# Four tiles for squares and for gated values, second products two steps later, in a fused convolution and two feed-forward layers

## The chip, the cores and the metric

The kernel runs on one core of a Trainium2 chip. The metric is the device time of one execution in microseconds; the time before is 761.09 us, the median of three runs (760.44 to 761.89). Lower is better.

## The reference

Two sequences of 4160 tokens with 192 channels pass through three layers, all in float32:

```python
# 1: a convolution over the last 7 tokens, with weights per token and head (8 heads)
w = exp(weight_gen - max); w = w / (sum(w) + 1e-9)
x = einsum("bshk,bskhg->bshg", w, last_7_tokens(x))
# 2: feed-forward, 192 -> 1024 -> 192, with the token before mixed in
xk = mu_k * x + (1 - mu_k) * x_prev;  xr = mu_r * x + (1 - mu_r) * x_prev
k = maximum(xk @ w_k, 0)
x = sigmoid(xr @ w_r) * (k * k @ w_v)
# 3: feed-forward, 192 -> 1024 -> 192, with a gate from a convolution over 3 tokens
h = maximum(x @ w_in, 0)
out = (h * sigmoid(conv3(h, conv_w))) @ w_out
```

## The kernel before, in words

**Tiles and steps.** The sequence is cut into ten tiles (256, 220, seven of 476, and 352 tokens), and every tile is worked for both sequences: a tile and a sequence make a unit. In a unit the 1024 hidden channels are done in eight steps of 128, numbered `fi`. A float32 product is made of five matmuls on values split into a high and a low part.

**One step of layer 2** (`moe1`, lines 600 to 636): the first product, five matmuls of `wkA` and `wkB` into a PSUM bank `pa` (two banks); ScalarE takes relu and square in place (`c1`, `c2`) and copies the high part into a tile `s` (`c3`); VectorE subtracts and writes the low part into the same tile (`c4`), which frees the bank; the second product (`go2`, `out_passes`), five matmuls of `wv`, adds the tile `s` into the banks `am` and `ar`. There are two tiles `s`.

**One step of layer 3** (`moe2`, lines 695 to 751): the first product, five matmuls of `wiA` and `wiB` into a bank `pc` (two banks); ScalarE makes `h` (relu) and starts the convolution in the bank (`c1`, `c2`), VectorE adds two taps, ScalarE takes the sigmoid (`c5`), VectorE multiplies by `h` in the bank (`c6`), ScalarE copies the high part into a tile `g` (`c7`) and VectorE writes the low part (`c8`), which frees the bank; the second product, five matmuls of `wo`, adds the tile `g` into the banks `bm` and `br`. There are two tiles `g`.

**Between the layers** `mix_out` multiplies `am` and `ar` by the gate `r` and writes the input `x` of layer 3, and `store` sends the result out. GpSimd does the convolution of layer 1 (`prod`, `tok`) and the low parts of the inputs of layer 2 (`xA`, `mk`). Once for seven of the tiles ScalarE takes an Exp over a 128x2576 block of weights, with a table load before and after.

**What sets the order.** All operations are recorded first, each with a planned time in steps: `at(t, ...)`, where a unit begins at `T + 8 * b` with `T = 16 * i`, step `fi` of layer 2 at `t + fi`, and the same step of layer 3 `LAG` later. Tiles and banks are given out in the order of these planned times (`Ring`, `Shift`). `Program.schedule` then plays the operations through a table of costs: every engine takes, of its operations whose inputs are ready, the one with the lowest planned time. The order that comes of it is fixed in the program; on the chip each engine goes through its list in order and waits where an input is late. `Shift` rings lend tiles after a planned time: for the last steps layer 3 gets the tiles `s` beside `g`, the banks `pa` beside `pc`, and the tiles `mk` beside `h`.

All recorded operations carry line 176 in the profile, so groups are told apart by their tiles.

Of the kernel before, what the change touches and what calls it, by code (L numbers as in the profile page):

```python
# [9 lines left out]
F32R = mybir.dt.float32r  # L10
U32 = mybir.dt.uint32
ACTF = mybir.ActivationFunctionType
ALU = mybir.AluOpType
AX = mybir.AxisListType

NB, SEQ, DM, NH, KS, DFF = 2, 4160, 192, 8, 7, 1024
SIZES = [256, 220] + [476] * 7 + [352]
NTILE = len(SIZES)
STARTS = [sum(SIZES[:i]) for i in range(NTILE)]
NMAX = max(SIZES)  # L20
# [7 lines left out]
PAD = KS - 1  # L28
WIN = KS * DM
NF = DFF // 128  # L30
LAG = 10

DONE = 16 * NTILE + 0.3


def f(ap):
    return ap.bitcast(F32)
# [153 lines left out]
def conv_moe_kernel(ctx: ExitStack, tc: tile.TileContext, xp, wg_first, wg_rest, mus, w_k, w_v, w_r, w_in, conv_w, w_out, out):  # L191
    nc = tc.nc
    prog = Program(nc)
    PE, ACT, DVE, POOL, SP = (prog.engine(e) for e in ("PE", "ACT", "DVE", "POOL", "SP"))
# [8 lines left out]
    def ring(name, n, shape, dtype=F32):  # L203
        return Ring([new(f"{name}{j}", shape, dtype) for j in range(n)])
# [5 lines left out]

    W = NMAX + 4

    class Shift:


        def __init__(self, own, lent, till=None, since=None):
            self.both, self.own, self.tiles, self.till, self.since = Ring(own + lent), Ring(own), own, till, since

        def __call__(self):
            if self.since is None:  # L220
                return self.both() if prog.now < self.till else self.own()
            if prog.now < self.since:
                return self.own()
            if not self.both.n:

                k = self.own.n % len(self.tiles)
                self.both.tiles = self.tiles[k:] + self.tiles[:k] + self.both.tiles[len(self.tiles):]
            return self.both()


    mu = new("mu", [128, 4])
# [15 lines left out]
    stage = new("stage", [128, 4096], U32)  # L247
# [2 lines left out]

    early = x2[1].rearrange("p a b -> p (a b)")
    wb_r = Ring([early[:, :1024].rearrange("p (a b) -> p a b", a=2)])
    g_r = ring("g", 2, [128, 2, W], F32R)
    wz_r = Ring([t.rearrange("p a b -> p (a b)") for t in g_r.tiles])
    rows_r = ring("rows", 2, [128, max(SLOTS) + PAD, DM])
    prod_r = ring("prod", 2, [128, WIN])
    tok_r = ring("tok", 2, [128, max(SLOTS), NB * DM])
# [1 line left out]
    mk_r = ring("mk", 2, [128, NMAX])  # L259
# [1 line left out]
    xA_r = [ring(f"xA{k}", 2, [128, 2, NMAX], F32R) for k in range(2)]  # L261
    xB_r = [ring(f"xB{k}", 3, [128, NMAX], F32R) for k in range(2)]
    r_r = [ring(f"r{k}", 1, [128, NMAX]) for k in range(2)]
    s_r = ring("s", 2, [128, 2, NMAX], F32R)
    h_r = ring("h", 2, [128, W])
    om_r = ring("om", 1, [128, W])

# [2 lines left out]
    soft_at = [sum(slots[:j]) for j in (0, 1, 2, 3, NTILE)]  # L270
# [14 lines left out]
    px_r = Ring([bm_r.tiles[0], br_r.tiles[0]])  # L285
    py_r = Ring(pc_r.tiles)

    pt_r = Shift(pc_r.tiles, pa_r.tiles, since=DONE)
    ht_r = Shift(h_r.tiles, mk_r.tiles, since=DONE)
    gt_r = Shift(g_r.tiles, s_r.tiles, since=DONE)  # L290

    plan = []

    def at(t, fn, hold=0.0):
        plan.append((t, len(plan), fn, hold))
# [304 lines left out]
    def moe1(i, b, fi, t):  # L600
        N = SIZES[i]
        st = {}
        sl = slice(128 * fi, 128 * fi + 128)

        def go():
            p = pa_r()
            st["p"] = p[:, :N]
            mm(st["p"], passes_in(wkA, wkB, xin[i, b, 0, 0], xin[i, b, 0, 1], sl, N))

        def c1():  # L610
            ACT.activation(st["p"], st["p"], ACTF.Relu)

        def c2():
            ACT.activation(st["p"], st["p"], ACTF.Square)

        def c3():
            s = s_r()
            st["s"] = s
            ACT.copy(s[:, 0, :N], st["p"])

        def c4():
            s = st["s"]
            DVE.tensor_tensor(s[:, 1, :N], st["p"], f(s[:, 0, :N]), op=ALU.subtract)

        def go2():
            if fi == 0:
                acc["m"] = am_r.tiles[0]
                acc["r"] = ar_r.tiles[0]
            out_passes(wv, fi, st["s"], N, acc["m"], acc["r"])

        at(t, go)
        at(t + 0.28, c1)
        at(t + 0.45, c2)
        at(t + 0.56, c3)
        at(t + 0.68, c4)
        at(t + 1.25, go2)

    def out_passes(W, fi, s, n, am, ar):
        s0, s1 = s[:, 0, :n], s[:, 1, :n]
# [55 lines left out]
    def moe2(i, b, fi, t):  # L695
        last = i == NTILE - 1
        N = UNIT[i] + (2 if last else 0)
        X = x2[b]
        st = {}
        sl = slice(128 * fi, 128 * fi + 128)  # L700

        def go():
            p = pt_r()
            st["p"] = p
            n = N + 2
            mm(p[:, :n], [(wiA[:, 0, sl], X[:, 0, :n]), (wiA[:, 1, sl], X[:, 0, :n]), (wiA[:, 0, sl], X[:, 1, :n]),
                          (wiB[:, 0, sl], X[:, 2, :n]), (wiB[:, 1, sl], X[:, 3, :n])])

        def c1():
            h = ht_r()  # L710
            st["h"] = h
            ACT.activation(h[:, :N + 2], st["p"][:, :N + 2], ACTF.Relu)

        def c2():
            ACT.activation(st["p"][:, :N], st["h"][:, 1:N + 1], ACTF.Copy, scale=cw[:, 1, fi:fi + 1])

        def tap(k, o):
            DVE.scalar_tensor_tensor(out=st["p"][:, :N], in0=st["h"][:, o:o + N], scalar=cw[:, k, fi:fi + 1],
                                     in1=st["p"][:, :N], op0=ALU.mult, op1=ALU.add)

        def c5():
            ACT.activation(st["p"][:, :N], st["p"][:, :N], ACTF.Sigmoid)

        def c6():
            DVE.tensor_tensor(st["p"][:, :N], st["h"][:, 1:N + 1], st["p"][:, :N], op=ALU.mult)

        def c7():
            g = gt_r()
            st["g"] = g
            ACT.copy(g[:, 0, :N], st["p"][:, :N])  # L730

        def c8():
            g = st["g"]
            DVE.tensor_tensor(g[:, 1, :N], st["p"][:, :N], f(g[:, 0, :N]), op=ALU.subtract)

        def go2():
            if fi == 0:
                acc2["m"] = bm_r()
                acc2["r"] = br_r()
            out_passes(wo, fi, st["g"], N, acc2["m"], acc2["r"])  # L740

        at(t + 0.5, go)
        at(t + 0.78, c1)
        at(t + 0.9, c2)
        at(t + 1.03, lambda: tap(0, 0))
        at(t + 1.17, lambda: tap(2, 2))
        at(t + 1.35, c5)
        at(t + 1.47, c6)
        at(t + 1.66, c7)
        at(t + 1.8, c8)  # L750
        at(t + 2.75, go2)

    def store(i, b, t):
        N = UNIT[i]
# [63 lines left out]
    a = slots[3]  # L818
# [6 lines left out]
    for i in range(NTILE):  # L825
        T = 16 * i
        if i:
            for b in range(NB):
                attention(i, b, T - 22 + 4.5 * b, T - 15 + 4.5 * b + (2 if i == 3 else 0), 1.125, POOL, (25.0 + 8 * b if i == 1 else 0.0, 0.0))
            for u, t in UNITS.get(i, ((0, T - 5), (2, T - 3.7), (1, T + 3))):  # L830
                mixing(i, u, t, 2.5)
        for b in range(NB):
            t = T + 8 * b
            carry(i, b, t + 7)
            for k in range(2):
                gate_r(i, b, k, t + 5.12 + k)
            for fi in range(NF):
                moe1(i, b, fi, t + fi)
                if i:
                    moe2(i, b, fi, t + fi + LAG)  # L840
            mix_out(i, b, t + 8.52)
            if i:
                store(i, b, t + LAG + 10.02)

    heapq.heapify(plan)
    while plan:
# [68 lines left out]
```

## Time and profile before

| | |
|---|---|
| time of three runs | 760.44, 761.09, 761.89 us |
| span of the profiled execution, from its first to its last instruction | 757.9 us |
| median of the runs less this span | 3.2 us |
| TensorE (matmul) busy | 715.6 us, 94% of the span, 3473 matmuls |
| ScalarE busy | 656.6 us, 87% |
| VectorE busy | 606.8 us, 80% |
| GpSimd busy | 492.4 us, 65% |
| granted TensorE clock, mean | 0.992 |

The execution that was profiled has no time of its own beside its span, so the 3.2 us between the span and the median of the runs is taken as what lies around the span. A matmul is pipelined: its record lasts longer than the distance to the next one, so a busy TensorE can still have waited a little. GpSimd is busy nearly without a break until about 510 us, when the convolution of the last tile is done, and rests after that.

### The profile page before, as it was taken

The page shows a single profiled execution, that of the slowest core. Times are in us where ns is not written, and L with a number is a line of the kernel's source. Part 1 is how long each engine was busy: PE and PEld are TensorE (multiplying, and loading weights), DVE is VectorE, ACT ScalarE, POOL GpSimd, SP SyncE. Part 2 cuts the span into 40 slices and gives each one's busy share as a digit, 9 for nine tenths or more (in the row PEclk, how much of TensorE's full clock was granted, in tenths as well). Part 3 has the DMA queues.
Part 4 walks back from the last instruction along what each step waited for, and adds up shares of the span by engine and source line. Part 5 has one row for each costly group of instructions (what it writes and reads, how often), then busy time and mean ns, then how long its engine had stood idle before and what let it go on. Part 6 is the DMA issues. An engine that isn't in the chain of part 4 may idle for free.

```text
span 757.9 us, 10505 instructions
## 1 busy us (share of the span) xinstructions
PE 715.6 (94%) x3473; PEld 607.1 (80%) x3473; DVE 606.8 (80%) x1033; ACT 656.6 (87%) x1388; POOL 492.4 (65%) x350
## 2 busy tenths in 40 slices
PE   4888888997999999999999999999999999999996
PEld 2666777786888888888888788888888888888974
DVE  5756868878997979797979787978797979787887
ACT  2687689989899999899989898999899989898886
POOL 3899999995999999999999999695201000110000
PEclk9899999999999999999999999999999999999999
DMA  7688212101211041013021211020002000200000
GB/s 236 163 262 214 74 53 51 54 20 65 59 53 45 28 124 43 29 53 86 38 72 52 74 48 62 6 72 1 19 2 72 1 20 1 59 3 17 20 1 29
DMA packets 18790, 45.08 MB, mean 59 GB/s; under 512 B 2992, under 2 KB 14256, under 8 KB 18608
## 3 DMA queue, kind: packets, MB, share of 16 engines
q1 hardware_dynamic: 18736, 44.41, 19.8%
q8 instruction: 27, 0.44, 0.2%
q14 instruction: 27, 0.22, 0.1%
HBM read 27.40 MB, written 6.39 MB: 45 GB/s over the span
## 4 chain that ended last, share of the span: by engine, by line
PE 59%; POOL 20%; ACT 11%; DVE 6%; issue 3%; DMA 1%; SPq 0%; ACTq 0%; POOLq 0%; DVEq 0%
PE pa L176 18%; POOL prod L176 16%; PE pc L176 13%; PE bm L176 9%; PE am L176 8%; PE br L176 5%; PE ar L176 5%; ACT pa L176 2%; POOL tok L176 2%; ACT pc L176 2%; DVE pc L176 1%; POOL xA L176 1%; DVE stage L176 1%; ACT h L176 1%; ACT att L176 1%
## 5 line engine op out<-in xcount | busy, mean ns | idle before, releaser
L176 POOL TENSOR_TENSOR prod<-rows,sw 128x1344 f32<-128x1344 f32 x70 | 216.4, 3093 | 12.0 <-DVE sw L176 9.7
L176 DVE SCALAR_TENSOR_TENSOR pc<-h,cw,pc 128x476 f32<-128x476 f32 (+1 forms) x280 | 196.4, 702 | 29.5 <-ACT pc L176 27.0
L176 ACT ACTIVATE pa<-pa 128x476 f32<-128x476 f32 (+3 forms) x324 | 162.6, 504 | 38.2 <-PE pa L176 34.4
L176 POOL TENSOR_TENSOR prod<-prod 128x576 f32<-128x576 f32 (+1 forms) x132 | 161.6, 1224 | 8.8
L176 PE MATMUL am<-s,wv 128*128 128x476 f32 (+3 forms) x480 | 145.4, 362 | 8.3 <-ACT s L176 8.2
L176 PE MATMUL bm<-g,wo 128*128 128x476 f32 (+1 forms) x417 | 138.2, 378 | 4.1 <-ACT g L176 3.6
L176 PE MATMUL pa<-xA,wkA 128*128 128x476 f32 (+3 forms) x480 | 122.8, 360 | 3.6 <-DVE s L176 1.8
L176 DVE TENSOR_TENSOR pc<-h,pc 128x476 f32<-128x476 f32 (+1 forms) x140 | 90.0, 643 | 42.5 <-ACT pc L176 42.1
L176 POOL TENSOR_TENSOR xA<-mk,xA 128x476 fp32r<-128x476 f32 (+2 forms) x36 | 40.2, 1124 | 119.6 <-ACT xA L176 119.6
L176 PE MATMUL pc<-x,wiA 128*128 128x478 f32 (+1 forms) x420 | 115.4, 376 | 0.6 <-DVE g L176 0.5
L176 DVE TENSOR_TENSOR s<-pa,s 128x476 fp32r<-128x476 f32 (+3 forms) x162 | 94.9, 586 | 25.2 <-ACT s L176 23.0
L176 PE MATMUL ar<-s,wv 128*128 128x476 f32 (+3 forms) x320 | 109.4, 353 | 0.0
L176 PEld LDWEIGHTS am<-s,wv 128*128 128x128 f32 x480 | 86.3, 188 | 24.8 <-ACT s L176 14.1
L176 PE MATMUL br<-g,wo 128*128 128x476 f32 (+1 forms) x278 | 104.1, 375 | 0.0
L176 DVE TENSOR_TENSOR g<-pc,g 128x476 fp32r<-128x476 f32 (+1 forms) x137 | 87.6, 640 | 17.1 <-ACT g L176 16.6
L176 PEld LDWEIGHTS pa<-xA,wkA 128*128 128x128 f32 x480 | 84.8, 190 | 18.5 <-DVE s L176 3.9
L176 ACT ACTIVATE pc<-h,cw 128x476 f32<-128x476 f32 (+1 forms) x140 | 92.4, 660 | 1.6
L176 PEld LDWEIGHTS bm<-g,wo 128*128 128x128 f32 x417 | 76.9, 188 | 18.5 <-ACT g L176 6.4
L176 ACT ACTIVATE h<-pc 128x478 f32<-128x478 f32 (+1 forms) x140 | 79.8, 570 | 12.0 <-PE pc L176 9.1
L176 PE MATMUL pa<-xB,wkB 128*128 128x476 f32 (+3 forms) x320 | 88.8, 356 | 0.0
L176 PEld LDWEIGHTS pc<-x,wiA 128*128 128x128 f32 x420 | 76.2, 188 | 13.5 <-DVE g L176 2.5
L176 ACT CAST s<-pa 128x476 fp32r<-128x476 f32 (+3 forms) x162 | 83.5, 517 | 2.7 <-PE ar L176 0.8
(134 smaller groups left out, 1110.7 us busy)
## 6 DMA issues: line engine op xcount, KB each, us to landing
rows<-in_x_dram SPq DMA_DIRECT2D x14, 960.0 KB, 4.6
xB<-rm SPq DMA_DIRECT2D x28, 119.0 KB, 2.3
xB<-mk SPq DMA_DIRECT2D x28, 119.0 KB, 2.3
out_dram<-om SPq DMA_DIRECT2D x14, 238.0 KB, 2.0
rows<-in_x_dram SPq DMA_DIRECT2D x4, 768.0 KB, 6.0
rows<-in_x_dram SPq DMA_DIRECT2D x2, 864.0 KB, 4.4
out_dram<-att SPq DMA_DIRECT2D x14, 119.0 KB, 2.2
stage<-in_moe_w_v_dram SPq DMA_DIRECT2D x4, 384.0 KB, 4.6
```

Of the source, the lines that this page charges most:

```text
L176: getattr(self.real[eng], method)(*a, **k)
```

## The change

Layer 2 and layer 3 get four tiles `s` and four tiles `g`. Second products are planned two steps later in both layers (`S_LAG` 1.25 to 3.25, `G_LAG` 2.75 to 4.75), with `mix_out` and `store` moved by the same, and layer 3 starts one step later behind layer 2 (`LAG` 10 to 11). From tile 7 on, the gated value is written to a tile in SBUF (`q_r`, two tiles in the unused part of `stage`) and not back to its bank, and GpSimd makes the low part of it in place of VectorE. `Grow` replaces `Shift` for lending tiles, and lends the banks `pa` and the tiles `mk` 0.3 steps earlier. The scratch for DMAs is set to 1024 bytes.

```diff
-LAG = 10
-
-DONE = 16 * NTILE + 0.3
+LAG = 11
+
+S_LAG, G_LAG = 3.25, 4.75
+DONE = 16 * NTILE + S_LAG - 0.95
+ALONE = 7
...
+    class Grow:
+
+        def __init__(self, tiles, *more):
+            self.tiles, self.n, self.more = list(tiles), 0, list(more)
 
         def __call__(self):
...
+            while self.more and prog.now >= self.more[0][0]:
+                k = self.n % len(self.tiles)
+                self.tiles = self.more.pop(0)[1] + self.tiles[k:] + self.tiles[:k]
+                self.n = 0
+            self.n += 1
+            return self.tiles[(self.n - 1) % len(self.tiles)]
...
-    g_r = ring("g", 2, [128, 2, W], F32R)
-    wz_r = Ring([t.rearrange("p a b -> p (a b)") for t in g_r.tiles])
+    g_r = ring("g", 4, [128, 2, W], F32R)
+    wz_r = Ring([t.rearrange("p a b -> p (a b)") for t in g_r.tiles[:2]])
...
-    s_r = ring("s", 2, [128, 2, NMAX], F32R)
+    s_r = ring("s", 4, [128, 2, NMAX], F32R)
...
-    pt_r = Shift(pc_r.tiles, pa_r.tiles, since=DONE)
-    ht_r = Shift(h_r.tiles, mk_r.tiles, since=DONE)
-    gt_r = Shift(g_r.tiles, s_r.tiles, since=DONE)
+    spare = f(stage)[:, 2 * (soft_at[4] - soft_at[3]) * NH:]
+    q_r = Ring([spare[:, j * W:(1 + j) * W] for j in (0, 1)])
+    pt_r = Grow(pc_r.tiles, (16 * NTILE, pa_r.tiles))
+    ht_r = Grow(h_r.tiles, (16 * NTILE, mk_r.tiles))
+    gt_r = Grow(g_r.tiles, (DONE, s_r.tiles))
...
-        at(t + 1.25, go2)
+        at(t + S_LAG, go2)
...
         def c6():
-            DVE.tensor_tensor(st["p"][:, :N], st["h"][:, 1:N + 1], st["p"][:, :N], op=ALU.mult)
+            st["q"] = q_r() if i >= ALONE else st["p"]
+            DVE.tensor_tensor(st["q"][:, :N], st["h"][:, 1:N + 1], st["p"][:, :N], op=ALU.mult)
...
-            ACT.copy(g[:, 0, :N], st["p"][:, :N])
+            ACT.copy(g[:, 0, :N], st["q"][:, :N])
...
-            DVE.tensor_tensor(g[:, 1, :N], st["p"][:, :N], f(g[:, 0, :N]), op=ALU.subtract)
+            (POOL if i >= ALONE else DVE).tensor_tensor(g[:, 1, :N], st["q"][:, :N], f(g[:, 0, :N]), op=ALU.subtract)
...
-        at(t + 2.75, go2)
+        at(t + G_LAG, go2)
...
-            mix_out(i, b, t + 8.52)
+            mix_out(i, b, t + S_LAG + 7.27)
             if i:
-                store(i, b, t + LAG + 10.02)
+                store(i, b, t + LAG + G_LAG + 7.27)
...
-    nc = _bacc.Bacc("TRN2", target_bir_lowering=False, num_devices=1)
+    nc = _bacc.Bacc("TRN2", target_bir_lowering=False, num_devices=1, dynamic_dma_scratch_size=1024)
```

TensorE's list has the same matmuls in both kernels, in another order. In the middle of the program (tile 4; the number after a tile's name tells the buffer, `s_103` and `s_104` are the two tiles `s`) it reads before:

```order
L176 MATMUL pa_110<-xA_91,wkA 128x476 x3
L176 MATMUL pa_110<-xB_96,wkB 128x476 x2
L176 MATMUL am<-s_103,wv 128x476 x2
L176 MATMUL ar<-s_103,wv 128x476
L176 MATMUL am<-s_103,wv 128x476
L176 MATMUL ar<-s_103,wv 128x476
L176 MATMUL pc_112<-x_1_75,wiA 128x478 x3
L176 MATMUL pc_112<-x_1_75,wiB 128x478 x2
L176 MATMUL bm<-g_78,wo 128x476 x2
L176 MATMUL br<-g_78,wo 128x476
L176 MATMUL bm<-g_78,wo 128x476
L176 MATMUL br<-g_78,wo 128x476
```

Here a second product reads the square of the step just before. Behind the change the same place (`s_105` to `s_108` are the four tiles `s`) reads:

```order
L178 MATMUL pa_114<-xA_93,wkA 128x476 x3
L178 MATMUL pa_114<-xB_98,wkB 128x476 x2
L178 MATMUL am<-s_105,wv 128x476 x3
L178 MATMUL ar<-s_105,wv 128x476 x2
L178 MATMUL pc_115<-x_1_75,wiA 128x478 x3
L178 MATMUL pc_115<-x_1_75,wiB 128x478 x2
L178 MATMUL bm<-g_77,wo 128x476 x2
L178 MATMUL br<-g_77,wo 128x476
L178 MATMUL bm<-g_77,wo 128x476
L178 MATMUL br<-g_77,wo 128x476
L178 MATMUL am<-s_106,wv 128x476 x2
L178 MATMUL ar<-s_106,wv 128x476
```

The second products now read squares that are three steps old. Counted through the list, from the last matmul of a step's first product to its second product there were about 24 matmuls in layer 2 and 42 in layer 3 in the middle of the program, and there are now about 65 and 85. From the last `wv` matmul of a unit to the first `wiA` matmul of the same unit there were 42, and there are now 25.

ScalarE's list around the large Exp (`sw` 128x2576, in tile 3) reads before:

```order
L176 CAST s_103<-pa_110 128x476
L176 ACTIVATE pc_112<-pc_112 128x476
L176 ACTIVATE h_105<-pc_111 128x478
L176 ACTIVATE pc_111<-h_105,cw 128x476
L176 CAST g_78<-pc_112 128x476
L176 ACT_TABLE_LOAD
L176 ACTIVATE sw<-sw 128x2576
L176 COPY att_85<-pa_110 128x476
L176 ACTIVATE pa_109<-pa_109 128x476
L176 ACT_TABLE_LOAD
L176 ACTIVATE pc_111<-pc_111 128x476
```

And behind the change:

```order
L178 CAST s_105<-pa_113 128x476
L178 ACTIVATE h_110<-pc_116 128x478
L178 CAST g_77<-pc_115 128x476
L178 ACTIVATE pc_116<-h_110,cw 128x476
L178 ACT_TABLE_LOAD
L178 ACTIVATE sw<-sw 128x2576
L178 ACTIVATE pa_113<-pa_113 128x476
L178 CAST rm_91<-mk_89 128x476
L178 ACT_TABLE_LOAD
L178 ACTIVATE pc_116<-pc_116 128x476
L178 ACTIVATE r_103<-pa_114 128x476
```

The copies of the inputs of tile 3 (`att`, `xA`) now stand ahead of the Exp, and at the Exp two more tiles `s` and two more tiles `g` hold values whose second products are still to come.

VectorE's list at the end of the program reads before:

```order
L176 TENSOR_TENSOR g_78<-pa_110,g_78 128x354
L176 TENSOR_TENSOR pc_111<-h_105,pc_111 128x354
L176 SCALAR_TENSOR_TENSOR pc_112<-h_106,cw,pc_112 128x354
L176 TENSOR_TENSOR g_77<-pc_111,g_77 128x354
L176 TENSOR_TENSOR pc_112<-h_106,pc_112 128x354
L176 TENSOR_TENSOR s_103<-pc_112,s_103 128x354
L176 TENSOR_TENSOR att_86<-br,att_86 64x353
```

And behind the change:

```order
L178 TENSOR_TENSOR stage<-mk_89,pa_113 128x354
L178 SCALAR_TENSOR_TENSOR pa_114<-mk_90,cw,pa_114 128x354
L178 SCALAR_TENSOR_TENSOR pc_116<-h_110,cw,pc_116 128x354 x2
L178 TENSOR_TENSOR stage<-mk_90,pa_114 128x354
L178 TENSOR_TENSOR stage<-h_110,pc_116 128x354
L178 TENSOR_TENSOR att_88<-br,att_88 64x353
```

The low parts (`g<-pc,g`, `s<-pc,s`) are gone from VectorE's list: in tiles 7 to 9 there are 48 of them on GpSimd's, each reading `stage`, the tile of the gated value. Behind the last first product of layer 2 (`wkB`) TensorE's list had 130 matmuls, 33 of them ahead of the first matmul of the last unit's layer 3; it now has 160, with 69 ahead.

## Rows read from the trace of the kernel before

**Rows 1.** The page: span.
```profile
span 757.9 us, 10505 instructions
```

**Rows 2.** Windows: length, busy us of PE, PEld, DVE, ACT, POOL (instructions); PEclk, DMA, GB/s.
```profile
0.00:80.00 80.00, 60.97 (x309) 46.86 (x309) 50.98 (x110) 50.72 (x142) 62.45 (x49) 0.96 0.74 212
80.00:176.00 96.00, 88.32 (x477) 75.01 (x478) 77.53 (x135) 83.09 (x196) 92.47 (x66) 1.00 0.15 49
200.00:720.00 520.00, 516.85 (x2450) 444.76 (x2449) 428.60 (x696) 473.78 (x952) 323.49 (x226) 1.00 0.14 41
511.68:587.18 75.50, 75.22 (x354) 64.57 (x354) 61.84 (x99) 69.19 (x138) 19.06 (x15) 1.00 0.09 23
```

**Rows 3.** Chain that ended last, at 250 us: start, us, what.
```profile
250.13 1.08 PE pa L176 x5
```

**Rows 4.** Waits of weight loads (PEld), 200 to 720 us: us, times, longest.
```profile
PEld am L176 <- ACT s L176: 5.0, 8, 0.8
PEld pa L176 <- DVE s L176: 2.1, 8, 0.3
PEld pa L176 <- DVE mk L176: 1.4, 1, 1.4
PEld br L176 <- ACT g L176: 0.7, 2, 0.4
```

**Rows 5.** The same, 80 to 176 us.
```profile
PEld am L176 <- ACT s L176: 2.1, 3, 0.9
PEld bm L176 <- ACT g L176: 1.9, 3, 0.8
PEld bm L176 <- DVE g L176: 1.3, 1, 1.3
```

**Rows 6.** Timeline around the Exp: start, us, engine, instruction.
```profile
177.46 1.28 ACT L176 ACT_TABLE_LOAD   x1
178.75 2.36 ACT L176 ACTIVATE sw<-sw 128x2576 f32<-128x2576 f32 x1
182.02 1.28 ACT L176 ACT_TABLE_LOAD   x1
185.31 1.01 PE L176 MATMUL am<-s,wv 128*128 128x476 f32 x2 [4.03 <-ACT s L176]
```

**Rows 7.** Windows around the Exp and of the last unit, columns as in group 2.
```profile
177.40:181.10 3.70, 3.70 (x20) 3.06 (x18) 1.48 (x3) 3.67 (x4) 0.91 (x2) 1.00 0.08 29
185.30:190.00 4.70, 4.70 (x16) 4.01 (x17) 4.22 (x8) 3.72 (x8) 2.69 (x3) 0.64 0.22 71
...
731.30:753.40 22.10, 19.61 (x98) 14.93 (x96) 20.13 (x42) 17.05 (x42) 0.00 (x0) 1.00 0.04 13
```

**Rows 8.** Groups on DVE, 731.3 to 753.4 us: xcount, busy us, mean ns, idle before.
```profile
L176 DVE TENSOR_TENSOR s<-pc,s 128x354 fp32r<-128x354 f32 x3 | 1.6, 523 | 0.7 <-ACT s L176 0.5
...
L176 DVE TENSOR_TENSOR s<-pa,s 128x354 fp32r<-128x354 f32 x2 | 1.0, 520 | 0.0
```

**Rows 9.** Groups by shape, 560 to 757 us.
```profile
L176 POOL TENSOR_TENSOR xA<-mk,xA 128x352 fp32r<-128x352 f32 x4 | 3.8, 951 | 42.1 <-ACT xA L176 42.1
L176 ACT CAST g<-pc 128x354 fp32r<-128x354 f32 x9 | 4.1, 458 | 1.6 <-DVE pc L176 1.6
L176 ACT CAST xA<-mk 128x352 fp32r<-128x352 f32 x4 | 1.9, 474 | 0.1
```

**Rows 10.** Timeline from the last wv matmul of a unit to its layer 3.
```profile
398.66 0.38 PE L176 MATMUL ar<-s,wv 128*128 128x476 f32 x1
...
402.35 0.65 DVE L176 TENSOR_TENSOR x<-ar,x 64x476 fp32r<-64x476 f32 x1
...
407.75 0.80 PE L176 MATMUL pc<-x,wiA 128*128 128x478 f32 x3
```

**Rows 11.** Timeline: low parts on GpSimd for tile 6, and their reader.
```profile
428.24 2.41 POOL L176 TENSOR_TENSOR mk<-mk,rm 128x476 fp32r<-128x476 f32 x2
...
436.83 0.59 PE L176 MATMUL pa<-xB,wkB 128*128 128x476 f32 x2
```

More of the change, by code (lines that the diff above doesn't have):

```diff
@@ L211, in conv_moe_kernel @@
     W = NMAX + 4
-    class Shift:
-        def __init__(self, own, lent, till=None, since=None):
-            self.both, self.own, self.tiles, self.till, self.since = Ring(own + lent), Ring(own), own, till, since
+    class Grow:
+        def __init__(self, tiles, *more):
+            self.tiles, self.n, self.more = list(tiles), 0, list(more)
         def __call__(self):
[L220 to L228, printed above, removed]
+            while self.more and prog.now >= self.more[0][0]:
[4 more added lines that the diff above has]
+            return self.tiles[(self.n - 1) % len(self.tiles)]
     mu = new("mu", [128, 4])
```

## The prediction

> **What bounds the kernel now.** I read the page first, then windows by stage, the waits of TensorE's weight loads, the timeline at the one long wait, and the last unit by itself.
>
> The span is 757.9 us [rows 1]; the median of the runs is 3.2 us longer, and I add that at the end. From 200 to 720 us TensorE is busy for 516.85 of 520 us at the full clock (1.00, the 2.4 GHz level), ScalarE for 473.78 [rows 2]. One product of five matmuls takes 1.08 us there [rows 3], 0.216 us a matmul. So in two thirds of the span the bound is TensorE's own rate, and the change, which leaves the number of matmuls as it is, can win only what TensorE waits for. There are four such places.
>
> First, small waits in this stretch: weight loads of second products waited 5.0 us for a square (`am <- ACT s`) and 0.7 us for a gated value, and those of first products 2.1 us for a bank that VectorE had to free and 1.4 us for an input [rows 4]. Second, 80 to 176 us, with the same kinds of wait: 2.1, 1.9 and 1.3 us on squares and gated values [rows 5], while TensorE is busy for 88.32 of 96 us [rows 2]. Third, one long stall: at 177.46 us ScalarE loads a table, takes the Exp, and loads the first table again until 183.3 us. TensorE had 20 matmuls in hand, then waited 4.03 us for a square [rows 6, 7]. After the wait its granted clock is 0.64 on the mean of 185.3 to 190 us, part of it at the 1.2 GHz level, and 16 matmuls take 4.70 us [rows 7]; at 0.216 us [rows 3] they would take 3.46. The stall costs 4.03 + 1.24 = 5.3 us. Fourth, the last unit: from 731.3 to 753.4 us VectorE is busy for 20.13 of 22.1 us, ScalarE for 17.05, and TensorE's 98 matmuls [rows 7] at 0.216 x 356/476 = 0.16 us need only 16. There VectorE is the bound.
>
> The first 80 us (TensorE 60.97 of 80, DMA share 0.74 [rows 2]) are loads and the conversion of weights.
>
> **Second products two steps later, four tiles.** By the two lists, about 65 matmuls lie between a first product and its second product in layer 2 (24 before), 85 in layer 3 (42 before). At 0.216 us that is 14 us in place of 5.2, and 18 in place of 9. ScalarE is busy for 69.19 us of a tile's 75.5 [rows 2], so a chain of three or four of its instructions is late by fractions of a microsecond, never by 9.
>
> From 200 to 720 us the 5.7 us of waits on second products should go. What is late next is the bank: `pa` and `pc` still have two banks each, the chain that frees them is untouched, and a wait on a square now hides part of the wait on the bank that follows it. I give 1.2 us back to the banks: 4.5 us won. Bounds: all 5.7 won; nothing won, if every wait moves to a bank.
>
> From 80 to 176 us the rows on second products add up to 5.3 us. The steps are shorter there, and the banks turn over faster against the same chain, so I take 2 us, with bounds of 0 and 5.3.
>
> At the Exp the new list of ScalarE has the inputs of tile 3 done before, and three squares and three gated values are waiting for their second products. Counted from the first product that ScalarE reads last before its table load, 36 matmuls stand in TensorE's list up to the first that needs a result from behind the Exp (the bank of the gate `r`). ScalarE has three instructions between that product and the table load; at 0.6 us each, an estimate from the copies' 458 ns on 354 columns [rows 9], that is 1.8 us or 8 matmuls. 28 are left, 6.0 us. From the table load to the second table's end took 5.84 us [rows 6], and a sigmoid and `r` follow, 1.2 us by the same estimate: a wait of some 1 us, and about 1 us more on the squares right behind. So 3.3 of 5.3 us go; with a shorter wait the clock should not fall as far. I take 3.5 us, with bounds of 0 (ScalarE reaches the Exp late, with its tiles drained) and 5.3.
>
> **`LAG`, `mix_out`, and the end.** Between a unit's last `wv` matmul and its first `wiA` matmul lie 25 matmuls, 5.4 us, in place of 42. The chain in between (VectorE, ScalarE, VectorE) took from 399.04 to 403.00 us, 4.0 us, and TensorE came to its reader only at 407.75 [rows 10]. The last part of `x` is read by the fifth matmul, 0.9 us later: 2.3 us are left. I price it at nothing; the 25 matmuls hide it. If they don't, it is the rival on the other side.
>
> After the last first product of layer 2 there are 160 matmuls, not 130, so it comes 30 x 0.16 = 4.8 us earlier, with 69 matmuls and not 33 until the last unit's layer 3. That is a shift of the same work, at nothing. In the last unit ten low parts leave VectorE, at 0.52 us (two of four rows stand here) 5.2 of 20.13 us [rows 7, 8]; 14.9 are left. ScalarE's 17.05 us are the bound then. With the same ratio of window to busiest engine (22.1 / 20.13) the window is 18.9 us: 3.2 less. The chain at the very end gets longer: a low part takes about 0.95 us on GpSimd [rows 9], not 0.52, and the last two come one behind the other: 0.4 + 0.5 us. The end wins 2.3 us; I take 2. Bounds: 4 us (VectorE's idle goes with its work), and a loss of 1, when each part is late by its longer time.
>
> [...]
>
> The copy of the high part now reads SBUF: 474 ns against 458 [rows 9], 10 x 0.016 = 0.2 us in the last unit, and hidden in TensorE's work in tiles 7 to 9 before. [...]
>
> **GpSimd's list, queues, scratch.** GpSimd's low parts for tiles 4 to 6 stand one convolution product earlier in its list than before, so they keep up with a TensorE that is a few us earlier: for tile 6 they ended at 430.65 us and were read, after a DMA, at 436.83 [rows 11]. Low parts for tile 2 stand behind two more weight products (2.3 us), and GpSimd's list ahead of them is the same. `store` moves with its product, and SP only issues DMAs. [...] I price these at nothing, with 2 us either way for the order of the first 80 us.
>
> **Sum.** 4.5 + 2 + 3.5 + 2 = 12 us. 757.9 - 12 = 745.9 us of span, and with 3.2 around it 749.1 us: I say 749.
>
> **Rivals.**
> Banks take the waits over: nothing is won from 80 to 176 and from 200 to 720 us, only at the Exp and the end: 761.1 - 5.5 = 755.6, 756 us. For it speak the 2.1 us on banks, against it that these are under half of the waits on squares [rows 4]. 0.16.
> More goes than I count: all of the 5.7, 5.3 and 5.3 us, 4 at the end, 2 in the first 80 us, 22 us: 739. 0.09.
> GpSimd's parts stand on the path of the end: each of the last ten is 0.43 us longer than on VectorE [rows 8, 9], 4.3 us lost in place of 2 won: 755. Against it: four tiles let the parts of neighbouring steps overlap, and GpSimd has nothing else to do there. 0.05.
> No change: the Exp still drains TensorE, banks take the small waits, and the longer parts eat the end's gain: 760 to 762. 0.07.
> Slower, by one mechanism: `mix_out` no longer fits under 25 matmuls. It costs nothing up to 2.3 us of delay, then 1 us a unit for each further us, in 17 units; at 3.5 us of delay 17 x 1.2 = 20 us, 761.1 - 12 + 20 = 769. It decides the sign from 3.0 us of delay on. For it speaks that VectorE and ScalarE have longer chains of other steps in their lists by then, against it that VectorE is idle for 13.7 of 75.5 us [rows 2]. 0.06.
>
> **Chances.** The forecast has 0.57. A measurement of this kernel tells about 0.2%, 1.5 us, from no change. Faster by more: 0.57 + 0.16 + 0.09 + 0.05 less a little for the weak end of the first rival, 0.86. Within: 0.08. Slower: 0.06. The forecast's own range is 744 to 754; the range reaches from the second rival to past the first and the third, with the 2 us on the first 80 us: 739 to 758.
>
> **What would show it.** Right: `am <- ACT s` on TensorE's weight loads from 200 to 720 us falls from 5.0 us to under 1; no wait of over 2 us and a clock of 0.9 or more in the windows at the Exp; a tile takes under 75.2 us; in the last unit ScalarE, not VectorE, is the busiest, and the window from its first `wiA` matmul to its last `wo` matmul is near 20 us. Wrong: `pa <- DVE s` or `pc <- DVE` waits grow by what `am` loses; waits of TensorE on `x` in every unit; low parts of `g` on GpSimd that TensorE waits for.

## The result, and the profile after

The changed kernel takes 749.06 us, the median of 4 runs (747.3 to 749.3); the kernel before took 761.24. The ratio is 0.984, with a 95% interval of 0.982 to 0.985. The profiled execution has a span of 747.5 us against 757.9, which is 10.4 less; its own time, 749.3 us, is 1.8 us longer than its span. In all runs of the two kernels and their variants below this difference is 1.7 to 2.2 us. So the execution that was profiled before took some 759.7 us, faster than the median, and of the 12.2 us between the two medians the two traces hold 10.4.

The windows of the changed kernel answer to [rows 2], the last of them to the third of [rows 7]; the columns are those of [rows 2]:

```profile
0.00:80.00 80.00, 60.52 (x315) 46.87 (x316) 50.95 (x111) 51.48 (x145) 62.40 (x50) 0.98 0.74 212
80.00:176.00 96.00, 89.46 (x480) 76.09 (x480) 78.55 (x138) 84.26 (x200) 91.91 (x64) 0.98 0.16 50
176.00:200.00 24.00, 22.89 (x104) 18.41 (x103) 21.92 (x35) 23.14 (x42) 16.74 (x14) 1.00 0.29 81
200.00:720.00 520.00, 517.32 (x2463) 446.94 (x2462) 411.21 (x666) 471.07 (x960) 365.12 (x262) 1.00 0.14 40
724.10:743.05 18.95, 16.85 (x93) 14.44 (x91) 14.50 (x29) 15.76 (x39) 9.40 (x10) 1.00 0.05 15
```

From 200 to 720 us TensorE is hardly busier than before (517.32 against 516.85). The last unit, from its first `wiA` matmul to its last `wo` matmul, is 3 us shorter, with 93 matmuls in its window in place of 98, and VectorE in it went from 20.13 to 14.50 us.

Fixed windows hide a shift, so I also set the two traces beside each other at equal work: each matmul counts with its columns, and the table gives the time at which the same share of all products has been started.

| stretch (time in before, us) | ahead at its end, us | won in it, us |
|---|---|---|
| start to 173 | 1.1 | 1.1 |
| 173 to 220, with the Exp | 6.0 | 4.9 |
| 220 to 301 | 5.8 | -0.2 |
| 301 to 341 | 1.9 | -3.9 |
| 341 to 665 | 4.4 | 2.5 |
| 665 to 707 | 5.4 | 1.0 |
| 707 to the end | 10.4 | 5.0 |

Where the order of the two lists differs, neighbouring points of this measure scatter, by a microsecond or two in the first 130 us. One loss of 3.9 us stands among the gains. The waits of weight loads from 200 to 720 us, as in [rows 4], show what ended them:

```profile
PEld pa L178 <- DVE s L178: 4.5, 9, 2.5
PEld pc L178 <- DVE g L178: 3.0, 12, 0.6
...
PEld pc L178 <- DVE stage L178: 0.7, 2, 0.5
```

`am <- ACT s`, 5.0 us before, is gone from the list. Waits on banks that VectorE frees are now the largest, and 2.5 us of them are one single wait. Before, the waits of `pc` on VectorE were these:

```profile
PEld pc L176 <- DVE g L176: 0.8, 3, 0.3
```

So `pa <- DVE s` grew by 2.4 us and `pc <- DVE` by 2.9, together 5.3 us, as much as `am` lost. The prediction had named this as a sign of being wrong. Around the single wait of 2.5 us, GpSimd, VectorE and TensorE stand like this (three timelines of the changed kernel: start, duration, instruction, and in brackets how long its engine had been idle and who ended that):

```profile
330.07 3.09 POOL L178 TENSOR_TENSOR prod<-rows,sw 128x1344 f32<-128x1344 f32 x1
333.12 2.34 POOL L178 TENSOR_TENSOR xA<-mk,xA 128x476 fp32r<-128x476 f32 x2
```

```profile
331.38 0.65 DVE L178 TENSOR_TENSOR pc<-h,pc 128x476 f32<-128x476 f32 x1
334.35 0.71 DVE L178 SCALAR_TENSOR_TENSOR mk<-att,onemu,pa 128x476 f32<-128x476 f32 x1 [2.33 <-POOL xA L178]
334.98 0.65 DVE L178 TENSOR_TENSOR s<-pa,s 128x476 fp32r<-128x476 f32 x1
```

```profile
335.68 1.27 PE L178 MATMUL pa<-xA,wkA 128*128 128x476 f32 x3 [2.09 <-DVE s L178]
```

Read from the top: GpSimd takes a weight product of 3.09 us before the low parts of `xA`. VectorE wants to write `mk`, of which there are two tiles, and GpSimd has yet to read the one whose turn it is. Behind that write, in VectorE's list, stands the low part of a square, and the bank that it frees is the one TensorE needs. When the wait ends, at 335.7 us, the granted clock falls: it is 0.50 from 336.05 to 339.46 us, and five matmuls over 476 columns, from 336.75 to 338.73 us, take 1.98 us there, where one such product took 1.08 before [rows 3]. These are 1.2 columns a ns, the prediction's 1.2 GHz level; its 2.4 is twice that, an estimate by the shares of 0.50 and 1.00. Two windows have the clock at 0.76 and 0.82 on the mean:

```profile
334.00:338.00 4.00, 2.32 (x7) 1.97 (x8) 3.62 (x6) 1.97 (x4) 4.00 (x5) 0.76 0.26 60
338.00:342.00 4.00, 4.00 (x17) 3.44 (x16) 2.06 (x4) 3.29 (x7) 3.92 (x5) 0.82 0.75 169
```

At the Exp two waits of TensorE's weight loads are left, 1.7 us together, and the clock stays at 1.00 (the window from 176 to 200 us above; 0.64 behind the stall before [rows 7]):

```profile
188.33 0.51 PEld L178 LDWEIGHTS pa<-xA,wrA 128*128 128x128 f32 x3 [1.27 <-ACT r L178]
189.71 0.30 PEld L178 LDWEIGHTS am<-s,wv 128*128 128x128 f32 x2 [0.44 <-ACT s L178]
```

### The profile page after: what moved, and what is told of

Same layout as the page of the kernel before. It is cut to its first block, busy times and chain, and to the rows that moved or that the text cites. A ratio compares the mean times of both kernels' runs of the same rounds, so it can differ in the third digit from the quotient of the medians.

```text
span 747.5 us, 10554 instructions
## 1 busy us (share of the span) xinstructions
PE 711.2 (95%) x3473; PEld 606.9 (81%) x3473; DVE 581.2 (78%) x985; ACT 650.0 (87%) x1388; POOL 546.7 (73%) x398
## 4 chain that ended last, share of the span: by engine, by line
PE 48%; POOL 35%; ACT 6%; DVE 4%; issue 4%; DMA 2%; SPq 0%; ACTq 0%; POOLq 0%; DVEq 0%
POOL prod L178 28%; PE pa L178 15%; PE pc L178 10%; PE bm L178 7%; PE am L178 6%; PE br L178 5%; PE ar L178 4%; POOL tok L178 3%; POOL xA L178 2%; DVE pc L178 1%; ACT pa L178 1%; POOL mk L178 1%; DMA stage<-in_moe_w_in_dram 1%; DMA stage<-in_moe_w_k_dram 1%; DVE mk L178 1%
## 5 line engine op out<-in xcount | busy, mean ns | idle before, releaser
L178 ACT ACTIVATE pa<-pa 128x476 f32<-128x476 f32 (+4 forms) x326 | 163.3, 504 | 29.6 <-PE pa L178 26.0
L178 PE MATMUL am<-s,wv 128*128 128x476 f32 (+3 forms) x480 | 142.0, 356 | 2.9 <-ACT s L178 2.8
L178 PE MATMUL bm<-g,wo 128*128 128x476 f32 (+1 forms) x414 | 135.2, 379 | 2.1 <-ACT g L178 1.8
L178 POOL TENSOR_TENSOR g<-stage,g 128x476 fp32r<-128x476 f32 (+1 forms) x42 | 48.5, 1156 | 96.3 <-ACT g L178 76.0
L178 PE MATMUL pc<-x,wiA 128*128 128x478 f32 (+1 forms) x414 | 113.4, 379 | 0.9 <-ACT x L178 0.4
L178 DVE TENSOR_TENSOR s<-pa,s 128x476 fp32r<-128x476 f32 (+3 forms) x160 | 93.8, 586 | 21.6 <-ACT s L178 20.2
L178 DVE TENSOR_TENSOR pc<-h,pc 128x476 f32<-128x476 f32 x96 | 62.8, 654 | 26.9 <-ACT pc L178 26.0
L178 PE MATMUL pc<-x,wiB 128*128 128x478 f32 (+1 forms) x276 | 81.7, 377 | 0.0
```

The costliest lines, as they stand in the source:

```text
L178: getattr(self.real[eng], method)(*a, **k)
```

## The experiments

Each ratio is to runs of the kernel before that were taken together with this one, with its 95% interval; the changed kernel's is 0.9836 (0.9822 to 0.9850). The medians of the kernel before in these groups lie between 760.65 and 761.24 us, so a difference of two medians from two groups can be off by some 0.6 us, and the ratios are the better comparison.

| kernel | median, us | ratio |
|---|---|---|
| tiles_alone | 762.68 | 1.0018 (1.0006 to 1.0031) |
| lags_alone | 766.22 | 1.0076 (1.0060 to 1.0092) |
| low_parts_alone | 755.69 | 0.9925 (0.9906 to 0.9944) |
| no_low_parts | 754.76 | 0.9902 (0.9881 to 0.9924) |
| own_tile_alone | 753.80 | 0.9903 (0.9885 to 0.9921) |
| third_mk | 749.46 | 0.9841 (0.9816 to 0.9867) |
| four_mk | 744.47 | 0.9788 (0.9771 to 0.9804) |
| four_mk_before | 758.87 | 0.9977 (0.9968 to 0.9987) |
| no_exp_before | 757.85 | 0.9961 (0.9945 to 0.9976) |
| no_exp_after | 747.16 | 0.9824 (0.9809 to 0.9839) |
| four_mk_from_6 | 747.04 | 0.9823 (0.9808 to 0.9839) |
| four_mk_four_q_from_6 | 744.17 | 0.9783 (0.9759 to 0.9807) |

### Which part carries how much

**tiles_alone**, against the changed kernel (the smaller scratch stays):

```diff
-LAG = 11
+LAG = 10
-S_LAG, G_LAG = 3.25, 4.75
+S_LAG, G_LAG = 1.25, 2.75
-ALONE = 7
+ALONE = 99
```

> Four tiles for squares and for gated values with the lags of before and no low parts on GpSimd; the lists of the engines are nearly those of before (75 rows of TensorE's 2038 differ). Theory (the lag carries the gain, the tiles only make room for it): am still follows its square by 1.25 steps, so TensorE's waits for the cast of the square, 5.0 us in 200 to 720, and the stall at the Exp stay. Time 759 to 761. Rival (the tiles carry it): casts run ahead by themselves, those waits fall by half or more, and the time is 753 to 756.

Measured: 762.68 us. The waits on squares from 200 to 720 us stand as they did in [rows 4]:

```profile
PEld am L178 <- ACT s L178: 5.0, 8, 0.8
```

Four tiles, together with `Grow` and the smaller scratch, win nothing: 0.2% is lost. What each of the three does alone is not shown.

**lags_alone**, against the changed kernel:

```diff
-ALONE = 7
+ALONE = 99
-g_r = ring("g", 4, [128, 2, W], F32R)
+g_r = ring("g", 2, [128, 2, W], F32R)
-s_r = ring("s", 4, [128, 2, NMAX], F32R)
+s_r = ring("s", 2, [128, 2, NMAX], F32R)
```

> The changed lags with two tiles for squares and two for gated values, and no low parts on GpSimd. Theory (lag needs the tiles): with two tiles a cast waits until the second product of two steps before has read its tile, and that product now stands two steps later; TensorE waits for squares and gated values all through, and the time is 765 to 800. Rival (the lag alone does it, since the order of TensorE's list is what counts): 753 to 756, as no_low_parts with 754.9.

Measured: 766.22 us, within what was expected, but not by the mechanism that I gave. With two tiles step f + 2 writes its square, in the recorded order, ahead of the second product of step f, which then reads the later step's square: this part of the computation is changed. TensorE does not wait for squares all through (2.1 us from 200 to 720) but for banks:

```profile
PEld pa L178 <- DVE s L178: 10.2, 16, 2.8
```

With another flow of data its time says nothing on lag by itself; it shows only that this lag needs more than two tiles.

**low_parts_alone**, against the changed kernel:

```diff
-LAG = 11
+LAG = 10
-S_LAG, G_LAG = 3.25, 4.75
+S_LAG, G_LAG = 1.25, 2.75
-    g_r = ring("g", 4, [128, 2, W], F32R)
+    g_r = ring("g", 2, [128, 2, W], F32R)
-    s_r = ring("s", 4, [128, 2, NMAX], F32R)
+    s_r = ring("s", 2, [128, 2, NMAX], F32R)
```

> The kernel before with one part of the change: from tile 7 on GpSimd makes the low parts of the gated values, out of a tile of their own; two tiles and the lags of before. Theory (the parts act on different places): the last unit shortens by 2 to 4 us, the Exp stall and the waits for the square before tile 7 stay; time 757 to 759. Rival (GpSimd's low part of 0.95 us is too late for second products that follow by 2.75 steps): TensorE waits for g in tiles 7 to 9, and the time is 761 or more.

Measured: 755.69 us, a gain of 5.4, more than the 2 to 4 expected. At equal work nothing is won before 665 us (0.5 behind), and 5.3 us are won from there on. In its last unit VectorE has 16.36 us of work in place of 20.13 [rows 7], and the window is 20.25 us:

```profile
728.40:748.65 20.25, 18.57 (x95) 14.98 (x95) 16.36 (x33) 17.55 (x43) 10.36 (x11) 1.00 0.05 15
```

**no_low_parts**, against the changed kernel:

```diff
-ALONE = 7
+ALONE = 99
```

> The changed kernel with the low parts of the gated values on VectorE in all tiles; tiles and lags as changed. Theory (GpSimd's low parts give the end): 18 to 20 low parts of 0.52 us return to VectorE in the last unit, where it is the busiest, and the last unit goes from 19.0 us back towards the 21.9 us of before; in tiles 7 and 8 TensorE's wait for the square returns to 0.7 us per tile. Time 752 to 753. Rival (the two steps of lag give the end): the last unit stays under 20 us and the time at 749 to 750.

Measured: 754.76 us, the median of five runs (a sixth, of 1166.74 us, is left out), 5.7 slower than the changed kernel and beyond the expectation. Its last unit takes 22.9 us, and the clock in it is not full:

```profile
726.40:749.30 22.90, 18.62 (x89) 16.31 (x87) 18.42 (x38) 15.64 (x37) 0.00 (x0) 0.85 0.04 13
```

One single wait is 3.5 us of this window, and it is on ScalarE: TensorE needs the bank `bm`, out of which ScalarE has still to copy the result of the unit before (`om`).

```profile
PEld bm L178 <- ACT om L178: 3.5, 1, 3.5
```

At equal work this trace keeps its distance to the changed kernel's from 640 to 724 us, and its whole loss comes behind that, where this wait and the slow clock stand. So the theory has the place right, but this run does not separate VectorE's load from that wait.

Tiles with lag are thus worth 6.4 us (761.12 - 754.76) and low parts on GpSimd 5.4 to 5.7; the sum, 12, is what both bring together. They act in different places.

**own_tile_alone**, against the changed kernel:

```diff
-            (POOL if i >= ALONE else DVE).tensor_tensor(g[:, 1, :N], st["q"][:, :N], f(g[:, 0, :N]), op=ALU.subtract)
+            DVE.tensor_tensor(g[:, 1, :N], st["q"][:, :N], f(g[:, 0, :N]), op=ALU.subtract)
```

> The changed kernel with VectorE making the low parts in all tiles, but from tile 7 on still out of a tile of its own in SBUF, so that the bank of PSUM is free before the low part. Theory (VectorE's work is what counts at the end): like no_low_parts, 754 to 755.5, last unit near 22.9 us. Rival (the bank that comes free earlier is what counts): the last unit stays under 20.5 us and the time is 749 to 751.

Measured: 753.80 us, just under the theory's range, and a ratio of 0.9903 against 0.9902 for no_low_parts. The bank that comes free earlier is worth nothing that can be measured. The profiled run, 750.4 us, is its fastest and looks like the rival: its last unit took 20.2 us, not 22.9, at a clock of 1.00, and against the changed kernel it loses 2.4 us in the last unit. Its clock over the whole span is 0.992, that of the five other runs 0.983 to 0.987, so a good part of what they take longer goes with the clock. Where they lost it is not shown.

### The loss at 330 us

**third_mk**, against the changed kernel; `spare` is the part of `stage` that lies idle from tile 4 on:

```diff
+    mk_own = mk_r.tiles
+    mk_r = Grow(mk_own, (16 * 4, [spare[:, 2 * W:2 * W + NMAX]]))
-    ht_r = Grow(h_r.tiles, (16 * NTILE, mk_r.tiles))
+    ht_r = Grow(h_r.tiles, (16 * NTILE, mk_own))
```

> The changed kernel, and from tile 4 on a third mk tile, laid in the part of stage that lies idle then; GpSimd's list keeps its prod instructions where they are. Theory (the two mk tiles): the 4 us that the changed kernel loses at 330 to 340 us come from VectorE's write of mk waiting 2.33 us for GpSimd's xA, which stands behind a prod of 3.09 us, with the square that frees a bank queued behind that write. With a third tile that wait goes, the granted clock there stays at 0.98 to 1.00, and the time falls by 3 to 4 us, to 745 to 746. Rival (GpSimd itself is late): the low part of xA is needed by TensorE soon after, so the wait moves to TensorE for xA and the time stays at 748 to 749.

Measured: 749.46 us, so the theory's time failed. The trace says why: at equal work the kernel is 2.4 us ahead of the changed one from 359 to 399 us, and level again at 420. A unit writes two `mk`, and two units follow each other closely, so four writes stand together; in the next tile the fourth of them met the same thing:

```profile
412.83 0.71 DVE L178 SCALAR_TENSOR_TENSOR mk<-att,onemu,pa 128x476 f32<-128x476 f32 x1 [3.09 <-POOL xA L178]
```

**four_mk**, against third_mk:

```diff
-    mk_r = Grow(mk_own, (16 * 4, [spare[:, 2 * W:2 * W + NMAX]]))
+    mk_r = Grow(mk_own, (16 * 4, [spare[:, 2 * W + j * NMAX:2 * W + (j + 1) * NMAX] for j in (0, 1)]))
```

> As third_mk, with a fourth mk tile beside the third. In third_mk the wait of VectorE at 330 us shrank from 2.33 to 0.6 us and TensorE was 2.4 us ahead from there to 399 us; at 412 us, in the next tile, the fourth write of mk met the same thing (3.09 us for xA behind a prod), and all was lost again. Theory (each write of mk that reuses a tile too soon can lose 2 to 4 us): with four tiles, as many as the two units next to each other write, both losses go, the clock stays at 1.00 through 326:346 and 400:420, and the time is 745 to 746. Rival (GpSimd's list is simply late, and any slack is used up by the next reader, rm or xA or TensorE itself): TensorE waits for xA or xB there instead, and the time stays at 748.5 to 749.5.

Measured: 744.47 us, a little beyond the theory's range, and 4.6 under the changed kernel (3.7 by the two ratios). No write of `mk` waits any more, and from 200 to 720 us TensorE is never idle:

```profile
200.00:720.00 520.00, 520.00 (x2496) 451.47 (x2495) 415.71 (x676) 474.35 (x969) 366.45 (x264) 1.00 0.14 40
```

**four_mk_before**, against the kernel before:

```diff
+    spare = f(stage)[:, 2 * (soft_at[4] - soft_at[3]) * NH + 2 * W:]
+    mk_own = mk_r.tiles
+    mk_r = Shift(mk_own, [spare[:, j * NMAX:(j + 1) * NMAX] for j in (0, 1)], since=16 * 4)
-    ht_r = Shift(h_r.tiles, mk_r.tiles, since=DONE)
+    ht_r = Shift(h_r.tiles, mk_own, since=DONE)
```

> The kernel before with four mk tiles from tile 4 on, and nothing else; TensorE's list is the same row for row. VectorE's writes of mk waited once for xA there, 1.2 us (3.5 us in three waits in the changed kernel). Theory (the loss on mk was brought by the change, whose list puts xA behind a prod): four tiles win 1 to 2 us here, 759 to 760, against 4.6 in the changed kernel. Rival (two mk tiles cost the same in both, and the change only showed it): 756 to 757.

Measured: 758.87 us, 2.1 less, against 4.6 in the changed kernel; by the ratios it is 0.23% against 0.48%. Before, one write of `mk` waited, at 400 to 425 us:

```profile
DVE mk L176 <- POOL xA L176: 1.2, 1, 1.2
```

With four tiles the trace wins 1.3 us between 422 and 463 us. So, as far as these intervals tell, close to half of what four tiles win was lost before the change already, and the change brought the other half.

### The price of the Exp

**no_exp_before** and **no_exp_after** are the kernel before and the changed one without one line:

```diff
-    at(45.3, lambda: ACT.activation(sm[3][0][:, a:], sm[3][0][:, a:], ACTF.Exp))
```

> The kernel before without the Exp over 128x2576 and the two table loads around it; the later tiles then use weights that are not normalised. In the changed kernel leaving it out gave 1.9 us. Theory (the stall costs its wait and the slow clock behind it, 4.03 + 1.24 us): 5 to 6 us less, 755 to 756. Rival (part of the stall comes back as later waits, or the first 176 us decide): 3.5 us less or under, 757 or more.

> The changed kernel without the Exp over 128x2576 at 177 us and without the two table loads around it; the later tiles then use weights that are not normalised. Theory (with the lag the Exp costs little): TensorE still waits 1 us or less around it, so the time falls by 0.5 to 1.5 us, to 747.5 to 748.5. Rival (the Exp still costs, hidden as a later wait of casts): it falls by 3 us or more, to 746 or less.

Measured: 757.85 us (3.1 less than before) and 747.16 (1.9 less than after). By times alone the first theory missed on both sides, and before the change the rival's 757 or more held. The traces separate the place from the rest. Without the Exp, the kernel before wins 5.5 us between 173 and 188 us, where the stall and the slow clock were priced at 5.3; but 2.0 us were lost ahead of it, where the list is another one too (VectorE is busy for 31.15 of 32 us from 130 to 162 us, 24.54 in the kernel before), and 1.2 us are lost later. In the changed kernel the same stretch, taken to 220 us, wins only 0.4 us; 2.6 us more are won in its trace at 330 us, where the wait on `mk` came out shorter. The clock agrees with this. From 176 to 200 us its mean is 0.93 in all four traces that have the Exp and the lags of before (before, tiles_alone, low_parts_alone, four_mk_before), and 1.00 in all seven that have the Exp, the new lags and four tiles. So the change takes away nearly all of the stall, and the difference of the two medians, 1.2 us, understates it, as leaving the Exp out moves other work too.

### A further step, and the same mechanism again

**four_mk_from_6**, against four_mk:

```diff
-ALONE = 7
+ALONE = 6
```

> four_mk (744.47 us) with GpSimd's low parts from tile 6 on and not from 7. Theory (the low parts pay where VectorE is late and GpSimd has nothing else, and by tile 6 TensorE is busy all the time): TensorE is busy for 520.00 of 520 us from 200 to 720, so nothing is left to win there; 744 to 745. Rival (GpSimd's prods and low parts collide in tile 6, as xA and prod did in tile 5): 746 to 748.

Measured: 747.04 us, 2.6 slower than four_mk; the rival was right. VectorE waited to write the tile of the product (`q`, in `stage`), two of which exist, for GpSimd's low part out of it, which again stood behind a weight product; TensorE's bank then came 1.82 us late. GpSimd's and VectorE's timelines:

```profile
487.63 3.09 POOL L178 TENSOR_TENSOR prod<-rows,sw 128x1344 f32<-128x1344 f32 x1
490.68 1.21 POOL L178 TENSOR_TENSOR g<-stage,g 128x476 fp32r<-128x476 f32 x1
```

```profile
491.93 0.65 DVE L178 TENSOR_TENSOR stage<-h,pc 128x476 f32<-128x476 f32 x1 [2.42 <-POOL g L178]
492.50 0.65 DVE L178 TENSOR_TENSOR s<-pa,s 128x476 fp32r<-128x476 f32 x1
```

**four_mk_four_q_from_6**, against four_mk_from_6 (the two `mk` tiles move up behind them):

```diff
-    q_r = Ring([spare[:, j * W:(1 + j) * W] for j in (0, 1)])
+    q_r = Ring([spare[:, j * W:(1 + j) * W] for j in range(4)])
```

> four_mk_from_6 (747.04 us) with four tiles in place of two for the product that GpSimd's low part reads; GpSimd's list is the same row for row. In four_mk_from_6 VectorE waited 2.42 us at 491.9 us to write such a tile, because GpSimd's low part out of it stood behind a prod of 3.09 us, and TensorE then 1.82 us for a bank. Theory (a tile that a late GpSimd instruction still reads holds up VectorE's list, and the banks behind it): both stalls go and the time is 744 to 745, that of four_mk. Rival (GpSimd's work in tile 6 is too much whatever the tiles): 746.5 to 747.5, with TensorE waiting for g.

Measured: 744.17 us with GpSimd's list unchanged. It was the number of tiles, not the amount of GpSimd's work:

```profile
200.00:720.00 520.00, 520.00 (x2497) 451.30 (x2495) 406.84 (x660) 474.75 (x970) 385.44 (x280) 1.00 0.13 40
```

It does not differ measurably from four_mk: from tile 6 on there was nothing left to win. Both beat the changed kernel by some 0.5%.

## Why the prediction was right, and which of its terms were not

The time came out as predicted, 749, but part of this is luck: the four terms were less good than their sum. At equal work 10.4 us were won, not 12. The Exp and the end, counted at 5.5, brought 9.9; the two stretches counted at 6.5 brought next to nothing. In the trace the condition of the first rival (nothing won there) thus held, and the time is not its 756 because the other two terms were too small. The 1.6 us that are missing from 12 do not show in the sum because of the 3.2 us that it adds around the span. No run shows this term: a run takes 1.8 us longer than its span, and the other 1.4 came from a profiled execution that was faster than the median.

- **200 to 720 us: 4.5 predicted.** The waits on squares went, as said (`am <- ACT s` from 5.0 us to none), and a tile takes 75.1 us (516.26 to 591.34 us, from first `wv` matmul to first `wv` matmul), under the 75.2 named. At equal work 0.6 us is lost from 220 to 707 us in all: 3.3 won, 3.9 lost at one place. The step that failed is "GpSimd's list, queues, scratch ... I price these at nothing". I had looked at who reads GpSimd's low parts, not at who writes the tiles that they read from. four_mk shows the price: 4.6 us with the tiles given (3.7 by the ratios), close to half of it lost in the kernel before as well.
- **Banks take the waits over (the first rival).** In the changed kernel they did: 5.3 us came back, 2.5 of them in the wait that the writing of `mk` brought. Without that it was in part, and as priced. In four_mk, with the loss gone, VectorE's low parts still hold `pa` for 1.4 us and `pc` for 2.6 from 200 to 720 us; before it was 2.1 [rows 4] and 0.8. So 1.1 us came back, where I had put 1.2.
- **80 to 176 us: 2 predicted, hardly anything seen in this trace.** The 1.1 us of the table count from the start, and at 80 us some 0.8 of them are there already. `am <- ACT s` rose, from 2.1 to 4.0 us, and the granted clock fell once, at 108 to 112 us (mean of the stretch 0.98, 1.00 before). four_mk has the same matmuls in the same order up to 200 us; its clock stayed at 1.00, it passes the changed kernel by 1.6 us at that place, and against the kernel before it wins some 1.5 us in the stretch. Before and four_mk_before, whose lists of matmuls are the same throughout, also part there by 1.5 us. So the term was near its size where the clock held, and how often it holds is not shown.
- **The Exp: 3.5 predicted, 4.9 seen.** The wait that I put at some 2 us was 1.7. The clock behind it, of which I counted only a part as won, did not fall at all, in this trace or in the six others with the same lags and tiles.
- **`mix_out` (the slower rival) did not come.** The chain after a unit's last `wv` matmul still took about 4 us, TensorE came to its reader 4.6 us after that matmul, and no product of layer 3 waited for `x` from 200 to 720 us.
- **The last unit: 2 predicted, 5.0 seen in the trace from 707 us on, 5.4 to 5.7 by the two runs on this part.** The window itself was forecast well: VectorE 14.9, measured 14.50; its length 18.9, measured 18.95. (17.05 x 22.1 / 20.13 is 18.7; 18.9 comes out with the 0.16 us of slower copies in it.) What was missing is the stretch ahead of it. In 26.1 us it holds 156 matmuls, where 26.4 us held 145 in the kernel before, and 11 at 0.16 us are 1.8 us (the changed kernel, then before):

```profile
698.00:724.10 26.10, 26.10 (x156) 25.56 (x155) 18.04 (x35) 22.59 (x55) 7.45 (x9) 1.00 0.05 15
705.20:731.60 26.40, 25.08 (x145) 23.32 (x145) 20.77 (x41) 23.11 (x55) 0.00 (x0) 1.00 0.05 15
```

  This is not the work of the low parts alone. With them on VectorE, no_low_parts has as many matmuls there:

```profile
700.00:726.40 26.40, 26.27 (x156) 25.54 (x156) 21.53 (x43) 22.28 (x55) 0.00 (x0) 1.00 0.05 15
```

  Either part of the change brings it: low_parts_alone, with the lags of before, holds 157 in the 26.4 us ahead of its last unit. And the longer chain at the very end, 0.9 us, did not show: from the last `wo` matmul to the end of the span it is 4.45 us in both traces.
- **The copy that reads SBUF: 16 ns more predicted, 32 seen.** On 354 columns it took 490 ns in the changed kernel against 458 before; the 474 that I had taken is that of another copy (`xA`) [rows 9]. On ten copies this is 0.3 us.
- **GpSimd's parts on the path of the end (the third rival).** No: TensorE's waits on them in the changed kernel add up to 1.2 us from 700 us on. Such a part takes 952 ns in the changed kernel against 520 on VectorE before [rows 8], and the move still won 5.4 to 5.7 us, where VectorE had been busy for 20.13 of 22.1 us [rows 7]. How much of that is VectorE's load, and how much single waits and the clock behind them, is not separated (no_low_parts, own_tile_alone).

## What to carry to other kernels

Work given to an engine with free time cost more here than its own duration: the tiles that it reads stay taken until its list comes to them (2.6 us in four_mk_from_6, gone with four tiles), so count who will write these tiles next, and what stands behind that write. Before moving or delaying such work, list for each ring of tiles the longest foreign instruction that can stand ahead of its last reader, and give the ring as many more tiles as are written in that time, out of memory that lies idle by then. Here more tiles by themselves won nothing, and the longer lag could not be had without them; and parts of a change are best priced place by place at equal work, as a right sum can hide a loss and a gain of the same size.

## What the runs showed of the hardware that was not expected

The same wait had two prices. Up to 200 us the changed kernel and four_mk have the same matmuls in the same order, and at one place the same wait (the changed kernel, then four_mk):

```profile
106.01 0.48 PE L178 MATMUL am<-s,wv 128*128 128x220 f32 x2 [1.28 <-ACT s L178]
106.97 0.48 PE L178 MATMUL am<-s,wv 128*128 128x220 f32 x2 [1.27 <-ACT s L178]
```

In the first the granted clock then fell, to 0.50 from 107.35 to 110.77 us, in the second it stayed at 1.00:

```profile
108.00:112.00 4.00, 4.00 (x17) 3.53 (x17) 1.71 (x4) 2.33 (x7) 3.77 (x5) 0.65 0.67 244
108.00:112.00 4.00, 4.00 (x25) 3.61 (x26) 2.92 (x6) 3.51 (x10) 3.76 (x4) 1.00 0.49 171
```

At equal work the second wins 1.6 us there. no_low_parts and own_tile_alone have the same lists around the wait on `mk`; TensorE waited 2.50 us for the bank in one and 2.30 in the other. In no_low_parts the granted clock then fell:

```profile
336.00:340.00 4.00, 3.10 (x9) 2.66 (x10) 3.37 (x6) 2.94 (x6) 4.00 (x4) 0.69 0.33 76
340.00:344.00 4.00, 4.00 (x18) 3.39 (x18) 1.87 (x3) 2.79 (x7) 3.92 (x4) 0.88 0.78 172
```

In own_tile_alone it stayed at 1.00:

```profile
332.00:336.00 4.00, 2.10 (x9) 1.30 (x9) 2.81 (x5) 1.59 (x4) 4.00 (x4) 1.00 0.07 18
336.00:340.00 4.00, 4.00 (x20) 3.45 (x20) 2.86 (x5) 3.86 (x9) 3.92 (x5) 1.00 0.76 170
```

Set beside each other at equal work, the second wins 1.6 us there. In third_mk an idle time of 2.90 us before a weight load also left the clock at 1.00, while behind the 4.03 us at the Exp it was 0.64 [rows 6, 7]. So in each pair a wait, of 1.3 us in one and of 2.3 to 2.5 in the other, cost 1.6 us more than itself in one of the two traces. The list of instructions alone does not decide it, as it is the same in each pair; what does, these runs do not tell.
